# The first two modulation rows of an adaLN block: two halves of 512 columns in place of four blocks of 256

## The chip, the cores and the metric

The kernel runs on one core of a Trainium2 chip. The time is the device time in microseconds (us) of one execution. A profile is one execution recorded by the hardware profiler; its times count from the start of its span, and lines such as L142 are lines of the kernel before.

## The reference

One transformer block, x of 2048 rows and D = 1024 columns, all in bf16. A condition vector c makes six modulation rows, two of which, `sa` (shift) and `ca` (scale), are needed before anything else:

```python
mod = (_silu(c) @ w_mod).reshape(c.shape[0], 6, 1, -1)
sa, ca, ga, sb, cb, gb = (mod[:, 0].copy(), mod[:, 1].copy(), mod[:, 2].copy(), mod[:, 3].copy(), mod[:, 4].copy(), mod[:, 5].copy())
h = _layernorm(x, axis=-1) * (1 + ca) + sa
x = x + ga * _A_ref(h, A_wqkv, A_wo)          # linear attention, 32 heads of 32
h = _layernorm(x, axis=-1) * (1 + cb) + sb
x = x + gb * _B_ref(h, B_w_gate, B_w_up, B_w_down)   # SwiGLU, F = 3584
```

In `_A_ref` the keys and queries go through phi(t) = t + 1 for t > 0, exp(t) otherwise; `kv` and `z` are sums over all rows, so the keys and values of all of x come first.

## The kernel before

The 2048 rows are four chunks of 512, each of four tiles of 128. `M4` holds the normalized, transposed and modulated x: for each chunk eight column blocks (`cc`, 128 features on the partitions) of 512 rows. After the start that this text is about, the order is: values (`v_group`, L257) and queries (`q_group`, L265) of chunk 0, keys and values of chunks 1 to 3 with the sums `kv_mm` (L274), the other queries, attention output (L466), then gate and up (L509, L515) and down (L534). All of it is written out in a list of labelled steps (`seq`, `after`) and emitted in that order; engines run their own instructions strictly in that order, and waits between engines are semaphores. The schedule is manual: nothing reorders it.

The start, up to the first value matmul, is code ahead of that list. Its parts:

- **Loads, all on the queue of SyncE (SP), in order.** c, four tiles of x (`load_x`, L137, 256 KB each), then `load_wme` (L142) and `load_wk` (L145) in turn. `wme` is an SBUF region for the 2048 columns of `w_mod` that make `sa` (columns 0 to 1023) and `ca` (1024 to 2047); `load_wme(p)` brings the 256 columns p of each, in two transfers of 512 KB, whose rows in memory are 512 bytes. `wk` are the key weights, 2 MB in rows of 2 KB, cut by column block: 0 and 1, 2 and 3, 4 and 5, 6, 7. Behind them stand the values' weights (`load_cols`, L148), the next four tiles of x and the queries' weights. A transfer waits on SP for the landing of the transfer eight before it.
- **Layer norm of the four tiles.** VectorE takes the statistics (`ln_stats`, L196 to L200), GpSimd the reciprocal root (L202, L204); `ln_xn` writes the normalized tile, on ScalarE (L214) for tiles 0, 1 and 3 and on GpSimd (L211) for tile 2.
- **Transposes.** `tr0(st)` (L326) turns a tile over on TensorE, eight transposes into bank `st` of PSUM; `tr0_evac(st)` copies them to `M4`, on ScalarE (L332) for tiles 0 and 2, on VectorE (L334) for tiles 1 and 3.
- **Modulation.** `mod_mm(p)` (L343) makes 256 columns of `ca` and of `sa` as columns of PSUM bank 7, 32 matmuls of one column each; `mod_rows(p)` copies them on VectorE (L349, L350) and adds 1 to the scale (L351); `modulate` (L224, VectorE) applies both to one column block of `M4` in place.
- **Keys of chunk 0.** Eight groups `G` = (tile, half of 512 columns), each a sum over the eight column blocks in a bank of its own: `kmm` (L242) is one matmul of 512 columns. Since a block p of modulation rows serves only two column blocks, seven groups run side by side in banks 0 to 6: all seven over column blocks 0 and 1, then 2 and 3, then 4 and 5, with the next block's `mod_mm` between their matmuls (at k == 10), and last each group over 6 and 7, with its evacuation `k_evac` (phi, L237 to L239) behind it. Bank 7 belongs to the modulation until then; group 7 follows as a whole.
- `warm(n)` (L187) issues n matmuls on zeros into bank 7: 21 at the very start, 3 between the transposes of tiles 0 and 1.

Of the kernel before, what the change touches and what calls it, by code (L numbers as in the profile page):

```python
# [21 lines left out]
def kernel(  # L22
# [13 lines left out]
    nc = tc.nc  # L36
    P = nc.NUM_PARTITIONS
    _, S, D = A_x.shape
# [3 lines left out]
    DC = D // P  # L42
# [4 lines left out]
    STC = SCW // P  # L47
    NB = 512
# [18 lines left out]
    wm_v = w_mod.rearrange("(p j) n -> p j n", j=DC)  # L67
    c_v = c.rearrange("o (p j) -> p (o j)", j=DC)
# [8 lines left out]
    bank = [psum.tile([P, NB], F32, name=f"bank{i}") for i in range(8)]  # L77
# [9 lines left out]
    def view(region, off, shape, dtype=BF16):  # L87
        n = 1
        for s_ in shape:
            n *= s_  # L90
        w = n * (2 if dtype == F32 else 1)
        ap = region[:, off:off + w]
        if dtype == F32:
            ap = ap.bitcast(F32)
        if len(shape) == 2:
            ap = ap.rearrange("p (a b) -> p a b", a=shape[0])
        elif len(shape) == 3:
            ap = ap.rearrange("p (a b c) -> p a b c", a=shape[0], b=shape[1])
        return ap
# [6 lines left out]
    wme = view(M3, 0, [DC, 2 * D])  # L106
# [24 lines left out]


    c_sb = const.tile([P, DC], BF16, name="c_sb")
    nc.sync.dma_start(out=c_sb[:], in_=c_v)

    def load_x(st):
        nc.sync.dma_start(out=xs[st % 6], in_=x2[st * P:(st + 1) * P, :])  # L137

    def load_wme(p):
        for base in (D, 0):  # L140
            s_ = slice(base + p * 256, base + (p + 1) * 256)
            nc.sync.dma_start(out=wme[:, :, s_], in_=wm_v[:, :, s_])  # L142

    def load_wk(c0, c1):
        nc.sync.dma_start(out=wk[:, c0:c1, :], in_=wqkv_v[:, c0:c1, D:2 * D])  # L145

    def load_cols(dst, base, h):
        nc.sync.dma_start(out=dst[:, :, h * NB:(h + 1) * NB],  # L148
                          in_=wqkv_v[:, :, base + h * NB:base + (h + 1) * NB])

    for st in range(STC):
        load_x(st)
    load_wme(0)
    load_wk(0, 2)
    load_wme(1)
    load_wk(2, 4)
    load_wme(2)
    load_wk(4, 6)
    load_wme(3)
    load_wk(6, 7)  # L160
    load_wk(7, 8)

# [9 lines left out]
    saT = const.tile([P, DC], BF16, name="saT")  # L172
    ca1T = const.tile([P, DC], BF16, name="ca1T")
    sbT = const.tile([P, DC], BF16, name="sbT")
    cb1T = const.tile([P, DC], BF16, name="cb1T")
    m1 = const.tile([P, 6, DC], BF16, name="m1")
# [5 lines left out]
    scT = const.tile([P, DC], BF16, name="scT")  # L182
    nc.scalar.activation(out=scT[:], in_=c_sb[:], func=ACT.Silu)

    def warm(n):
        for _ in range(n):
            nc.tensor.matmul(bank[7][:], lhsT=zt[:, 0:P], rhs=zt[:], start=True, stop=True)  # L187
# [4 lines left out]
    def ln_stats(st):  # L192
        x_sb = xs[st % 6]
        stats = small.tile([P, NH, nc.vector.BN_STATS_DIM], F32, name="stats")
        for i in range(NH):
            nc.vector.bn_stats(out=stats[:, i, :], in_=x_sb[:, i * NB:(i + 1) * NB])  # L196
        mv = small.tile([P, nc.vector.BN_AGGR_DIM], F32, name="mv")
        nc.vector.bn_aggr(out=mv[:], in_=stats[:])
        veps = small.tile([P, 1], F32, name="veps")
        nc.vector.tensor_scalar_add(out=veps[:], in0=mv[:, 1:2], scalar1=LN_EPS)  # L200
        rstd = small.tile([P, 1], F32, name="rstd")
        nc.gpsimd.tensor_tensor(out=rstd[:], in0=veps[:], in1=neg_half[:], op=ALU.pow)  # L202
        nmr = small.tile([P, 1], F32, name="nmr")
        nc.gpsimd.tensor_scalar(out=nmr[:], in0=mv[:, 0:1], scalar1=rstd[:], scalar2=-1.0,  # L204
                                op0=ALU.mult, op1=ALU.mult)
        stat[st] = (rstd, nmr)

    def ln_xn(st, pool):
        rstd, nmr = stat.pop(st)
        if pool:  # L210
            nc.gpsimd.tensor_scalar(out=xns[st % 6], in0=xs[st % 6], scalar1=rstd[:], scalar2=nmr[:],  # L211
                                    op0=ALU.mult, op1=ALU.add)
        else:
            nc.scalar.activation(out=xns[st % 6], in_=xs[st % 6], func=ACT.Identity, scale=rstd[:], bias=nmr[:])  # L214
# [7 lines left out]
    def modulate(sc_, cc, sT, c1T, c0=0, c1=SCW):  # L222
        h = M4[:, sc_, cc, c0:c1]
        nc.vector.tensor_scalar(out=h, in0=h, scalar1=c1T[:, cc:cc + 1], scalar2=sT[:, cc:cc + 1],  # L224
                                op0=ALU.mult, op1=ALU.add)
# [9 lines left out]
    def phi_to(dst, acc):  # L235
        e = epool.tile([P, NB], F32, name="e")
        nc.scalar.activation(out=e[:], in_=acc, func=ACT.Exp)  # L237
        nc.vector.tensor_scalar(out=e[:], in0=e[:], scalar1=1.0, scalar2=PHI_EPS, op0=ALU.min, op1=ALU.add)  # L238
        nc.vector.scalar_tensor_tensor(out=dst, in0=acc, scalar=0.0, in1=e[:], op0=ALU.max, op1=ALU.add)  # L239

    def kmm(acc, sc_, t, h, cc):
        nc.tensor.matmul(acc[:], lhsT=M4[:, sc_, cc, t * P:(t + 1) * P], rhs=wk[:, cc, h * NB:(h + 1) * NB],  # L242
                         start=(cc == 0), stop=(cc == DC - 1))

    def k_evac(acc, t, h):
        phi_to(pk[:, t, h * NB:(h + 1) * NB], acc[:])
# [76 lines left out]
    def tr0(st):  # L323
        tp = bank[st][:].bitcast(BF16).rearrange("p (c s) -> p c s", c=DC)
        for cc in range(DC):
            nc.tensor.transpose(tp[:, cc, :], xns[st][:, cc * P:(cc + 1) * P], ident[:])  # L326

    def tr0_evac(st):
        tp = bank[st][:].bitcast(BF16).rearrange("p (c s) -> p c s", c=DC)
        dst = M4[:, 0, :, st * P:(st + 1) * P]  # L330
        if st % 2 == 0:
            nc.scalar.copy(out=dst, in_=tp)  # L332
        else:
            nc.vector.tensor_copy(out=dst, in_=tp)  # L334

    def mod_mm(p):
        mps = bank[7][:, p * 4:p * 4 + 4]
        for kind, base in enumerate((D, 0)):
            for i in range(2):
                col = base + (2 * p + i) * P  # L340
                o = kind * 2 + i
                for j in range(DC):
                    nc.tensor.matmul(mps[:, o:o + 1], lhsT=wme[:, j, col:col + P], rhs=scT[:, j:j + 1],  # L343
                                     start=(j == 0), stop=(j == DC - 1))

    def mod_rows(p):
        mps = bank[7][:, p * 4:p * 4 + 4]
        c2 = slice(2 * p, 2 * p + 2)
        nc.vector.tensor_copy(out=m1[:, 1, c2], in_=mps[:, 0:2])  # L349
        nc.vector.tensor_copy(out=saT[:, c2], in_=mps[:, 2:4])  # L350
        nc.vector.tensor_scalar_add(out=ca1T[:, c2], in0=m1[:, 1, c2], scalar1=1.0)  # L351

    warm(21)
    for st in range(STC):
        ln_stats(st)
    ln_xn(2, True)
    mask = const.tile([P, KVW], BF16, name="mask")
    nc.gpsimd.memset(mask[:], 0.0)
    for j in range(HPC):
# [7 lines left out]
    ln_xn(1, False)  # L367
    tr0(1)
    tr0_evac(0)
    tr0_evac(1)  # L370
    mod_mm(0)
    mod_rows(0)
    modulate(0, 0, saT, ca1T, 0, 2 * P)
    modulate(0, 1, saT, ca1T, 0, 2 * P)
    tr0(2)
    ln_xn(3, False)
    load_cols(wv, 2 * D, 0)
    for st in range(STC, STC + 4):
# [1 line left out]
    load_cols(wv, 2 * D, 1)  # L380
    load_cols(wq, 0, 0)
    load_cols(wq, 0, 1)

    tr0_evac(2)
    G = [(t, h) for t in range(STC) for h in range(NH)]
    for g in (0, 1):
        for cc in (0, 1):
            kmm(bank[g], 0, G[g][0], G[g][1], cc)
    tr0(3)
    tr0_evac(3)  # L390
    modulate(0, 0, saT, ca1T, 2 * P, 4 * P)
    modulate(0, 1, saT, ca1T, 2 * P, 4 * P)
    for g in (2, 3):
        for cc in (0, 1):
            kmm(bank[g], 0, G[g][0], G[g][1], cc)
    mod_mm(1)
    mod_rows(1)
    for g in (4, 5, 6):
        for cc in (0, 1):
            kmm(bank[g], 0, G[g][0], G[g][1], cc)  # L400
    modulate(0, 2, saT, ca1T)
    modulate(0, 3, saT, ca1T)
    for p in (1, 2):
        k = 0
        for cc in (2 * p, 2 * p + 1):
            for g in range(7):
                kmm(bank[g], 0, G[g][0], G[g][1], cc)
                k += 1
                if k == 10:
                    mod_mm(p + 1)  # L410
                    mod_rows(p + 1)
                    modulate(0, 2 * p + 2, saT, ca1T)
                    modulate(0, 2 * p + 3, saT, ca1T)
    for g in range(7):
        for cc in (6, 7):
            kmm(bank[g], 0, G[g][0], G[g][1], cc)
        k_evac(bank[g], *G[g])
    for cc in range(DC):
        kmm(bank[7], 0, G[7][0], G[7][1], cc)
    k_evac(bank[7], *G[7])  # L420


    seq = []
# [264 lines left out]
```

## Time and profile before

| what | time |
|---|---|
| median of 4 runs | 848.64 us (848.32 to 849.03) |
| the profiled execution | 849.02 us, its span 847.2 us |
| first value matmul (L257) | 33.03 us |
| last modulation transfer: issued, landed | 17.54 us, 26.66 us |
| key matmul (L242), median | 379 ns; 216 ns from start to start where they follow each other |
| 32 modulation matmuls (L343) in a row | 0.80 us |
| `modulate`, 256 columns and 512 columns | 334 ns and 406 ns |
| granted clock of TensorE, mean | 0.997 |

The chain of waits follows the end of the program back to its start: at each step to what released it. A window's sum gives each engine's busy time in a stretch, the clock that TensorE was granted (1.00 is full speed), the mean busy share of the 16 DMA engines and what they moved. A matmul's time is its length from issue to its last result; matmuls overlap, so their distance from start to start tells what one costs.

### The profile page before, as it was taken

What the parts mean: (1) busy time and instruction counts of PE and PEld (TensorE: products, weight loads), DVE (VectorE), ACT (ScalarE), POOL (GpSimd) and SP (SyncE); (2) the same over time, 40 slices, a digit from 0 to 9 for tenths busy, and PEclk for the clock granted to TensorE, in tenths of its full rate; (3) what the DMA queues carried; (4) which work ended last, traced back from release to release, by engine and by line L of the source; (5) the groups of instructions that cost most, each with busy time, mean ns of one, the idle gap of its engine ahead of it and who ended that gap; (6) DMA issues with size and microseconds to landing.
All of it is one profiled execution on the core that took longest, in us unless ns stands there. A gap on an engine that the chain in (4) does not pass through costs nothing.

```text
span 847.2 us, 10893 instructions
## 1 busy us (share of the span) xinstructions
PE 834.7 (99%) x4368; PEld 396.6 (47%) x4452; DVE 323.5 (38%) x617; ACT 143.9 (17%) x269; POOL 80.0 (9%) x143
## 2 busy tenths in 40 slices
PE   8999999999999999999999999999999999999998
PEld 4444555544444444444444444444444444444444
DVE  5657365497755655422111121221122122112222
ACT  3333233322311111111111001111000111100000
POOL 2124030014122323100000000000000000000000
PEclk9999999999999999999999999999999999999999
DMA  9994982045499898777886215555322555301220
GB/s 285 308 242 114 283 191 69 1 116 159 99 213 216 217 218 213 194 246 238 242 240 180 69 52 168 151 150 149 106 75 69 151 153 158 86 18 64 75 69 26
DMA packets 203763, 128.65 MB, mean 152 GB/s; under 512 B 50496, under 2 KB 189888, under 8 KB 203712
## 3 DMA queue, kind: packets, MB, share of 16 engines
q1 hardware_dynamic: 163008, 98.58, 40.9%
q10 hardware_dynamic: 38400, 20.98, 11.1%
q0 software_dynamic: 2304, 8.39, 2.6%
q8 instruction: 35, 0.57, 0.3%
q14 instruction: 16, 0.13, 0.1%
HBM read 103.81 MB, written 12.58 MB: 137 GB/s over the span
## 4 chain that ended last, share of the span: by engine, by line
PE 95%; SPq 2%; DVE 1%; DMA 1%; issue 1%; ACT 0%; DVEq 0%
PE bank L515 23%; PE bank L534 23%; PE bank L509 23%; PE bank L466 7%; PE bank L265 6%; PE bank L257 6%; PE bank L242 5%; DMA M<-in_w_mod_dram 1%; SPq L145 1%; PE bank L439 1%; PE bank L274 1%; SPq L142 1%; PE bank L301 1%; DVE stats L196 0%; DVE M L239 0%
## 5 line engine op out<-in xcount | busy, mean ns | idle before, releaser
L515 PE MATMUL bank<-M,M 128*128 128x512 bf16 x881 | 210.4, 379 | 0.8
L509 PE MATMUL bank<-M,M 128*128 128x512 bf16 x871 | 209.7, 379 | 1.3
L517 DVE TENSOR_TENSOR M<-bank,e 128x512 bf16<-128x512 f32 x112 | 77.5, 692 | 275.1 <-PE bank L515 265.7
L534 PE MATMUL bank<-M,M 128*128 128x512 bf16 (+1 forms) x687 | 146.9, 370 | 0.6
L512 ACT ACTIVATE e<-bank 128x512 f32<-128x512 f32 x112 | 66.8, 597 | 439.7 <-PE bank L509 422.0
L534 PEld LDWEIGHTS <-M 128*128 128x128 bf16 x924 | 90.4, 98 | 103.2
L515 PEld LDWEIGHTS <-M 128*128 128x128 bf16 x896 | 87.7, 98 | 105.7
L509 PEld LDWEIGHTS <-M 128*128 128x128 bf16 x896 | 87.3, 98 | 103.8
L538 DVE TENSOR_TENSOR M<-bank,gb_bc 128x512 f32<-128x512 f32 (+1 forms) x33 | 22.3, 676 | 149.2 <-PE bank L534 135.3
L242 PE MATMUL bank<-M,M 128*128 128x512 bf16 x244 | 58.5, 383 | 0.9 <-issue 0.2
L466 PE MATMUL bank<-M,M 128*128 128x512 bf16 x254 | 57.8, 379 | 0.1
L265 PE MATMUL bank<-M,M 128*128 128x512 bf16 x250 | 56.7, 379 | 0.3
L257 PE MATMUL bank<-M,M 128*128 128x512 bf16 x250 | 56.2, 379 | 0.3
L237 ACT ACTIVATE e<-bank 128x512 f32<-128x512 f32 x64 | 37.8, 598 | 100.7 <-PE bank L265 48.4
L534 PE MATMUL bank<-M 128*128 128x512 bf16 x219 | 50.7, 379 | 0.3
L239 DVE SCALAR_TENSOR_TENSOR M<-bank,e 128x512 bf16<-128x512 f32 x64 | 44.3, 692 | 3.7
L238 DVE TENSOR_SCALAR e<-e 128x512 f32<-128x512 f32 x64 | 27.8, 434 | 41.5 <-ACT e L237 41.5
L466 PEld LDWEIGHTS <-M 128*128 128x128 bf16 x256 | 25.0, 98 | 29.7
L257 PEld LDWEIGHTS <-M 128*128 128x128 bf16 x256 | 24.7, 98 | 29.0
L242 PEld LDWEIGHTS <-M 128*128 128x128 bf16 x256 | 24.4, 99 | 28.4 <-DVE M L224 1.3
L265 PEld LDWEIGHTS <-M 128*128 128x128 bf16 x256 | 24.6, 98 | 27.9
L468 DVE TENSOR_TENSOR M<-bank,M 128x512 f32<-128x512 f32 x32 | 22.1, 690 | 14.5 <-PE bank L466 14.3
(66 smaller groups left out, 335.6 us busy)
## 6 DMA issues: line engine op xcount, KB each, us to landing
M<-in_B_w_gate_dram SPq DMA_DIRECT2D x56, 512.0 KB, 3.9
M<-in_B_w_up_dram SPq DMA_DIRECT2D x56, 512.0 KB, 5.0
M<-in_w_mod_dram SPq DMA_DIRECT2D x8, 1024.0 KB, 6.6
x_scratch<-M POOLq DMA_DIRECT2D x16, 512.0 KB, 5.8
M<-x_scratch ACTq DMA_DIRECT2D x16, 512.0 KB, 3.5
M<-in_B_w_down_dram SPq DMA_DIRECT2D x6, 1024.0 KB, 7.9
M<-in_A_x_dram SPq DMA_DIRECT2D x16, 256.0 KB, 6.8
M<-in_w_mod_dram SPq DMA_DIRECT2D x8, 512.0 KB, 8.0
```

Source lines behind the costliest of these rows:

```text
L237: nc.scalar.activation(out=e[:], in_=acc, func=ACT.Exp)
L238: nc.vector.tensor_scalar(out=e[:], in0=e[:], scalar1=1.0, scalar2=PHI_EPS, op0=ALU.min, op1=ALU.add)
L239: nc.vector.scalar_tensor_tensor(out=dst, in0=acc, scalar=0.0, in1=e[:], op0=ALU.max, op1=ALU.add)
L242: nc.tensor.matmul(acc[:], lhsT=M4[:, sc_, cc, t * P:(t + 1) * P], rhs=wk[:, cc, h * NB:(h + 1) * NB], start=(cc == 0), stop=(cc == DC - 1))
L257: nc.tensor.matmul(acc[:], lhsT=M4[:, sc_, cc, t * P:(t + 1) * P], rhs=wv[:, cc, h * NB:(h + 1) * NB], start=(cc == 0), stop=(cc == DC - 1))
L265: nc.tensor.matmul(acc[:], lhsT=wq[:, cc, qc * P:(qc + 1) * P], rhs=M4[:, sc_, cc, :], start=(cc == 0), stop=(cc == DC - 1))
L466: nc.tensor.matmul(acc[:], lhsT=oTs[st % 3][:, cc, :], rhs=wo[:, cc, hs], start=(cc == 0), stop=(cc == DC - 1))
L509: nc.tensor.matmul(g_ps[:], lhsT=wg_blk[:, cc, fs], rhs=M4[:, sc_, cc, :], start=(cc == 0), stop=(cc == DC - 1))
L512: nc.scalar.activation(out=sg[:], in_=g_ps[:], func=ACT.Silu)
L515: nc.tensor.matmul(u_ps[:], lhsT=wu_blk[:, cc, fs], rhs=M4[:, sc_, cc, :], start=(cc == 0), stop=(cc == DC - 1))
L517: nc.vector.tensor_tensor(out=gus[sc_][:, f, :], in0=u_ps[:], in1=sg[:], op=ALU.mult)
L534: nc.tensor.matmul(y_ps[:, 0:w], lhsT=gus[sc_][:, f, t * P:(t + 1) * P], rhs=wd(f)[:, c0:c1], start=(f == 0), stop=(f == FC - 1))
```

## The change

The modulation columns are loaded and used in two halves of 512: scale columns and shift columns of column blocks 0 to 3, then of 4 to 7. A transfer is 1,024 KB with rows of 1 KB. The key weights keep their five transfers, two behind the first half and three behind the second. The first tile of x is issued ahead of c.

On the engines: `mod_mm` and `mod_rows` take scale and shift apart (`kind` 0 and 1). Tile 2 is normalized on ScalarE; `ln_xn(2, False)` and `ln_xn(3, False)` stand behind `tr0_evac(0)` and ahead of `tr0_evac(2)` on that engine. All four tiles are transposed before the first key matmul, and two warm matmuls stand between. Then groups 0 to 3 run over column blocks 0 to 3, groups 4 to 6 over the same with the second half's scale matmuls ahead of the last block, then come the second half's shift matmuls, group 7 over blocks 0 to 3 in bank 7, and last all eight groups over blocks 4 to 7, each with its evacuation. The number of key matmuls (64) and of modulation matmuls (128) is the same.

```diff
--- before.py
+++ after.py
@@ -131,15 +131,13 @@
 
 
     c_sb = const.tile([P, DC], BF16, name="c_sb")
-    nc.sync.dma_start(out=c_sb[:], in_=c_v)
 
     def load_x(st):
         nc.sync.dma_start(out=xs[st % 6], in_=x2[st * P:(st + 1) * P, :])
 
-    def load_wme(p):
-        for base in (D, 0):
-            s_ = slice(base + p * 256, base + (p + 1) * 256)
-            nc.sync.dma_start(out=wme[:, :, s_], in_=wm_v[:, :, s_])
+    def load_wme(base, half):
+        s_ = slice(base + half * NB, base + (half + 1) * NB)
+        nc.sync.dma_start(out=wme[:, :, s_], in_=wm_v[:, :, s_])
 
     def load_wk(c0, c1):
         nc.sync.dma_start(out=wk[:, c0:c1, :], in_=wqkv_v[:, c0:c1, D:2 * D])
@@ -148,15 +146,17 @@
         nc.sync.dma_start(out=dst[:, :, h * NB:(h + 1) * NB],
                           in_=wqkv_v[:, :, base + h * NB:base + (h + 1) * NB])
 
-    for st in range(STC):
+    load_x(0)
+    nc.sync.dma_start(out=c_sb[:], in_=c_v)
+    for st in range(1, STC):
         load_x(st)
-    load_wme(0)
+    load_wme(D, 0)
+    load_wme(0, 0)
     load_wk(0, 2)
-    load_wme(1)
     load_wk(2, 4)
-    load_wme(2)
+    load_wme(D, 1)
+    load_wme(0, 1)
     load_wk(4, 6)
-    load_wme(3)
     load_wk(6, 7)
     load_wk(7, 8)
 
@@ -333,27 +333,25 @@
         else:
             nc.vector.tensor_copy(out=dst, in_=tp)
 
-    def mod_mm(p):
-        mps = bank[7][:, p * 4:p * 4 + 4]
-        for kind, base in enumerate((D, 0)):
-            for i in range(2):
-                col = base + (2 * p + i) * P
-                o = kind * 2 + i
-                for j in range(DC):
-                    nc.tensor.matmul(mps[:, o:o + 1], lhsT=wme[:, j, col:col + P], rhs=scT[:, j:j + 1],
-                                     start=(j == 0), stop=(j == DC - 1))
-
-    def mod_rows(p):
-        mps = bank[7][:, p * 4:p * 4 + 4]
-        c2 = slice(2 * p, 2 * p + 2)
-        nc.vector.tensor_copy(out=m1[:, 1, c2], in_=mps[:, 0:2])
-        nc.vector.tensor_copy(out=saT[:, c2], in_=mps[:, 2:4])
-        nc.vector.tensor_scalar_add(out=ca1T[:, c2], in0=m1[:, 1, c2], scalar1=1.0)
+    def mod_mm(kind, c0, c1):
+        for cc in range(c0, c1):
+            o = (2 * cc) + kind
+            col = (0 if kind else D) + cc * P
+            for j in range(DC):
+                nc.tensor.matmul(bank[7][:, o:o + 1], lhsT=wme[:, j, col:col + P], rhs=scT[:, j:j + 1],
+                                 start=(j == 0), stop=(j == DC - 1))
+
+    def mod_rows(kind, c0, c1):
+        src = bank[7][:, 2 * c0 + kind:2 * c1 + kind:2]
+        if kind:
+            nc.vector.tensor_copy(out=saT[:, c0:c1], in_=src)
+        else:
+            nc.vector.tensor_copy(out=m1[:, 1, c0:c1], in_=src)
+            nc.vector.tensor_scalar_add(out=ca1T[:, c0:c1], in0=m1[:, 1, c0:c1], scalar1=1.0)
 
     warm(21)
     for st in range(STC):
         ln_stats(st)
-    ln_xn(2, True)
     mask = const.tile([P, KVW], BF16, name="mask")
     nc.gpsimd.memset(mask[:], 0.0)
     for j in range(HPC):
@@ -367,12 +365,7 @@
     ln_xn(1, False)
     tr0(1)
     tr0_evac(0)
-    tr0_evac(1)
-    mod_mm(0)
-    mod_rows(0)
-    modulate(0, 0, saT, ca1T, 0, 2 * P)
-    modulate(0, 1, saT, ca1T, 0, 2 * P)
-    tr0(2)
+    ln_xn(2, False)
     ln_xn(3, False)
     load_cols(wv, 2 * D, 0)
     for st in range(STC, STC + 4):
@@ -380,44 +373,42 @@
     load_cols(wv, 2 * D, 1)
     load_cols(wq, 0, 0)
     load_cols(wq, 0, 1)
-
+    mod_mm(0, 0, 4)
+    tr0(2)
+    tr0_evac(1)
     tr0_evac(2)
+    mod_rows(0, 0, 4)
+    warm(2)
+    for c0 in (0, 2):
+        mod_mm(1, c0, c0 + 2)
+        mod_rows(1, c0, c0 + 2)
+        if c0 == 0:
+            tr0(3)
+        for cc in (c0, c0 + 1):
+            modulate(0, cc, saT, ca1T, 0, 2 * P)
+    tr0_evac(3)
+    for cc in range(4):
+        modulate(0, cc, saT, ca1T, 2 * P, 4 * P)
     G = [(t, h) for t in range(STC) for h in range(NH)]
-    for g in (0, 1):
-        for cc in (0, 1):
+    for cc in range(4):
+        for g in range(4):
             kmm(bank[g], 0, G[g][0], G[g][1], cc)
-    tr0(3)
-    tr0_evac(3)
-    modulate(0, 0, saT, ca1T, 2 * P, 4 * P)
-    modulate(0, 1, saT, ca1T, 2 * P, 4 * P)
-    for g in (2, 3):
-        for cc in (0, 1):
+    for cc in range(4):
+        for g in range(4, 7):
             kmm(bank[g], 0, G[g][0], G[g][1], cc)
-    mod_mm(1)
-    mod_rows(1)
-    for g in (4, 5, 6):
-        for cc in (0, 1):
-            kmm(bank[g], 0, G[g][0], G[g][1], cc)
-    modulate(0, 2, saT, ca1T)
-    modulate(0, 3, saT, ca1T)
-    for p in (1, 2):
-        k = 0
-        for cc in (2 * p, 2 * p + 1):
-            for g in range(7):
-                kmm(bank[g], 0, G[g][0], G[g][1], cc)
-                k += 1
-                if k == 10:
-                    mod_mm(p + 1)
-                    mod_rows(p + 1)
-                    modulate(0, 2 * p + 2, saT, ca1T)
-                    modulate(0, 2 * p + 3, saT, ca1T)
-    for g in range(7):
-        for cc in (6, 7):
+        if cc == 2:
+            mod_mm(0, 4, 8)
+            mod_rows(0, 4, 8)
+    mod_mm(1, 4, 8)
+    mod_rows(1, 4, 8)
+    for cc in range(4, 8):
+        modulate(0, cc, saT, ca1T)
+    for cc in range(4):
+        kmm(bank[7], 0, G[7][0], G[7][1], cc)
+    for g in range(8):
+        for cc in range(4, 8):
             kmm(bank[g], 0, G[g][0], G[g][1], cc)
         k_evac(bank[g], *G[g])
-    for cc in range(DC):
-        kmm(bank[7], 0, G[7][0], G[7][1], cc)
-    k_evac(bank[7], *G[7])
 
 
     seq = []
```

## The prediction

> **What bounds the kernel now.** I read the page's busy shares first, then the chain of waits over the first 60 us, then the sums by window for the DMA rate and the granted clock, then the timeline.
>
> ```profile
> span 847.2 us, 10893 instructions
> PE 834.7 (99%) x4368; PEld 396.6 (47%) x4452; DVE 323.5 (38%) x617; ACT 143.9 (17%) x269; POOL 80.0 (9%) x143
> ```
>
> TensorE is busy 99% of the span, so the change can only move what TensorE waits for before it streams. That is the start. The chain of waits, columns start, length, what:
>
> ```profile
> 16.95 0.54 SPq L142
> 17.50 0.04 issue
> 17.54 9.11 DMA M<-in_w_mod_dram
> 26.66 0.05 issue
> 26.70 0.55 PE bank L343 x16
> 27.25 0.89 PE bank L242 x4
> 28.14 0.03 issue
> 28.17 1.36 PE bank L242 x5
> 29.52 0.05 issue
> 29.58 3.62 PE bank L242 x16
> 33.19 7.12 PE bank L257 x33
> ```
>
> The last quarter of the two modulation rows is issued at 17.54 and lands at 26.66; behind it stand 16 modulation matmuls, a short wait for `modulate`, and the last key matmuls. From L257 on (the values of chunk 0; the timeline has the first at 33.03) the chain is TensorE without a gap of any size, to the end. So the change is worth what it does to one number, **the start of the first value matmul, now 33.03 us**. Nothing after it is edited: the same number of transfers, in the same order, follows.
>
> The whole start is fed by one stream of transfers. Columns below: window, length, busy us of PE, PEld, DVE, ACT, POOL (with counts), granted clock, DMA share, GB/s.
>
> ```profile
> 6.00:23.00 17.00, 14.76 (x166) 8.81 (x166) 9.03 (x29) 6.91 (x6) 5.18 (x19) 0.90 1.13 317
> 54.00:61.00 7.00, 6.95 (x34) 3.17 (x33) 6.29 (x17) 2.44 (x5) 0.00 (x0) 1.00 1.07 353
> 9.63:13.04 3.41, 1.82 (x46) 1.65 (x47) 2.95 (x9) 2.02 (x2) 2.54 (x7) 1.00 1.14 322
> 13.04:16.46 3.42, 3.20 (x19) 1.97 (x18) 0.38 (x1) 2.29 (x2) 0.63 (x9) 0.50 1.13 328
> ```
>
> A DMA share over 1 means that the queue is full: the stream runs at its own speed. In 6 to 23 us it moves rows of 512 bytes (modulation) and 2 KB (key weights); in 54 to 61 us it moves the late modulation loads of L293, rows of 1 KB from the same tensor, and is faster. The last two rows are for the clock, below.
>
> **The change, part by part.**
>
> *1. Rows of 1 KB.* The three late loads of L293 are issued at 50.54, 51.19 and 51.90 and land after 6.7, 9.1 and 11.3 us, at 57.2, 60.3 and 63.2: 3.0 us for each MB (1,024 KB). The rows before: the second load of block 0 lands at 10.67 (issued 3.77, 6.9 us), that of block 3 at 26.66. In these 16.0 us three blocks and three 512 KB pieces of key weights pass. A key piece takes 1.5 us at 353 GB/s (0.524 MB), which makes 4.5; one 16 KB instruction fetch lies in the queue near 17.4 us, and its packet lasts 1.2. That leaves 10.3 us, 3.43 for each MB. Saved: 0.43 to 0.45 a MB, for four MB **1.8 us**.
> Here a rule can be weighed against the row. The Trainium skill, "DMA: Bandwidth & Descriptors", section "Why small descriptors are slow (HBM only)", charges about 3 cycles for each packet on top of 32 bytes a cycle. By that 512 bytes cost 19 cycles and 1 KB costs 35, and a MB would go from 3.43 to 3.43 × 35/38 = 3.16 us: an estimate of 1.1 us saved in all. The sum below would come out at 848.8 in place of 848.1. I take the row: same tensor, same rows, same queue.
>
> *2. Order.* The last modulation piece now has one 512 KB key piece less ahead of it (1.0 MB in place of 1.5), 1.5 us. It lands at 26.66 − 1.8 − 1.5 = **23.35**. The last key rows, L145, land now at 27.96 (issued 23.36, 4.6 us); they gain only the 1.8, **26.15**. The first half lands later than block 0 did: its scale row at 10.67 − 0.45 = 10.2, its shift row 3.0 later at 13.2.
>
> *3. What follows the last modulation piece.* 32 matmuls of one column take 0.80 us (17.25 to 18.05 in the timeline). The copy of the row starts 0.20 after the last one and takes 0.16; bank 7 is free 0.06 later: 0.05 + 0.78 + 0.42 = 1.25 from landing. Four key matmuls into bank 7 (0.216 each, start to start) give 0.86, under which the four `modulate` of 512 columns run (0.33 apart, first from 1.25). The fourth is ready at 2.7 and its first user comes at 2.76, so nothing is left over. Then 32 key matmuls, 6.9. Sum: landing + 9.0 = **32.35**. This is longer than the 6.37 us behind the last landing now, since four column blocks of all eight groups wait in place of two of seven and a whole group.
>
> *4. The last key rows.* Group 0 needs column block 7 at once: 26.15 + 0.05 + 29 matmuls × 0.216 = **32.46**.
>
> *5. The first half on TensorE.* c_v moves behind the first tile of x: that tile is issued 0.45 earlier, and the normalization with it, except that the 21 warm matmuls end at 8.19 as now. Tile 2's normalization moves from GpSimd to ScalarE, behind the copy of tile 0's transposes and ahead of tile 3's: copy until about 10.1, then 1.24 and 1.24 more, ending near 11.3 and 12.6. So the 32 scale matmuls run 10.25 to 11.05, tile 2's transposes to 11.8, the two warm matmuls to 12.2, then a wait for 13.2. Shift matmuls, tile 3's transposes, shift matmuls: to 14.5 (14.9 with the transposes at half clock). The key matmul into bank 3 waits for VectorE, where two row copies, four `modulate` of 256 columns (0.33) and the 0.69 us copy of tile 3 are queued in that order: 16.4 to 16.75. Three key matmuls fit in ahead of it. The four remaining `modulate` end by 18 and are covered by 13 key matmuls (2.8 us). From there 22 key matmuls 4.75, 32 scale matmuls 0.80 (their half landed near 20.4), three key matmuls 0.65: TensorE is at the last shift row at **22.65 to 22.95**, 0.4 to 0.7 before it lands. With no wait at all this path would give 31.65 to 31.95.
>
> *6. Small parts.* The four fewer transfers cost nothing on SP, which is not late. The eight evacuations come every 0.86 us while VectorE needs 1.06 for each (29.54 to 30.61 in the timeline); the last ends near 36 us, now 38.1; bank 4, the last that a value group claims, is free long before its turn. The values' weights land now at 32.1, 0.9 us before use; they move up by 1.8 as well.
>
> **Sum.** The latest of 31.95, 32.35 and 32.46 sets the start: 32.46 − 33.03 = −0.57 us. The profiled execution took 849.02 (span 847.2 and 1.8 around it), and would be 848.45; the median of the runs is 848.64, 0.38 lower than that execution, and the difference goes off it: **848.1 us**. A measurement of this kernel can tell about 0.2%, 1.7 us, from no change; this is inside.
>
> **The rivals.**
>
> *A. One half-clock window more.* The row 9.63 to 13.04 holds 32 one-column matmuls, 14 transposes and a 1.4 us gap, and the next 3.42 us ran at 0.50. The Trainium skill, "TensorE: Matmul & The Clock Gate", section "HAM oscillation", gives as its rule no gaps over about 3.4 us; by that the new order, with no gap over 1.1 us, would never slow down. The row contradicts it, and speaks against this change: here the gap was 1.4. Between 21.2 and 24.5 the new kernel has 64 one-column matmuls, about a microsecond of waiting and only three key matmuls, a mix like that of the throttled row. A half-clock window there costs 3.41/2 = 1.7 us, fully on the path: 849.8. If instead the early one lasts past 16.4, to 19.9, TensorE is 1.7 late and the landing hides 0.4 to 0.7: about 849.2. Both are within 0.2%.
>
> *B. The slower side: the half clock holds for two windows behind the second half.* 3.4 us lost, 851.5. It decides when more than 1.7 + 0.57 = 2.3 us are lost, 1.35 windows. Against it: once the key matmuls flow, one busy window lifted it at 16.46.
>
> *C. The rows don't help.* If 1 KB rows go no faster at this crowded place, the last shift row lands at 25.15, plus 9.0: 34.15, 849.8. Against it: the row of 54 to 61 us.
>
> *D. The faster side.* The engine that the fetch delays by 1.2 us is what lands last. If the fetch falls elsewhere, shift row and key rows land at 22.1 and 24.9, and the first half too comes up to a microsecond sooner (shift row 12.2, TensorE ready at 21.9): 22.1 + 9.0 = 31.1, −1.9 us, 846.7.
>
> **How the numbers follow.** Forecast 0.48 (own range 847.3 to 849.0), A 0.15, C 0.08, B 0.16, D 0.13. Same: 0.48 + 0.15 + 0.08 = 0.71; slower 0.16; faster 0.13. The range reaches from D's 846.5 to the upper end of A and C, 850.2, and leaves out B.
>
> **What would show it.** First L257 matmul near 32.5; last shift row landing near 23.4 and the last key rows near 26.1; DMA about 350 GB/s from 6 to 24 us; granted clock 1.0 from 20 us on. I am wrong if the clock is 0.5 anywhere behind 20 us, if TensorE reaches the last shift row after it has landed, or if the landings haven't moved.

## The result

| | before | changed |
|---|---|---|
| median | 848.69 us (52 runs) | 849.85 us (34 runs) |
| lowest and highest | 848.12 to 849.31 | 848.04 to 850.89 |
| ratio, 95% interval | | 1.0012, 1.0007 to 1.0017 |
| profiled execution, its span | 849.02, 847.2 | 849.49, 847.7 |
| first value matmul | 33.03 | 33.23 |

The changed kernel is slower by 0.12%. That is less than the 0.2% that I had called the limit of what can be told, but clear of its interval: the forecast of 848.1 missed by 1.75 us, and in sign. The spread is as telling: the kernel before stays within 1.2 us, the changed one covers 2.9. Grouped by the mean granted clock that each execution reports, the 34 fall apart:

```
mean granted clock    executions    median us
0.997 and 0.998            9          848.78
0.995 and 0.996           25          850.07
```

One stretch of 3.41 us at half clock lowers the mean over 847 us by 0.002, so the second row is one such stretch more, and it comes with 1.3 us. The page of the changed kernel's profile has almost the same busy shares as before:

```profile
span 847.7 us, 10891 instructions
PE 834.6 (98%) x4370; PEld 396.5 (47%) x4454; DVE 323.0 (38%) x614; ACT 145.4 (17%) x270; POOL 78.9 (9%) x142
```

The chain of waits of the changed kernel's first 60 us (start, length, what; L341 is now the modulation matmul, L347 the copy of a shift row):

```profile
3.77 10.00 DMA M<-in_w_mod_dram
13.77 0.05 issue
13.82 0.59 PE bank L341 x16
14.40 0.88 PE bank L326 x8
...
16.52 0.61 DVE M L334
17.13 0.04 issue
17.17 2.36 PE bank L242 x6
...
22.99 0.78 PE bank L341 x32
23.77 0.45 PE bank L242 x2
24.22 0.05 issue
24.27 0.96 PE bank L341 x32
...
29.35 4.05 PE bank L242 x18
33.40 6.69 PE bank L257 x31
```

The last landing that the chain follows is now that of the **first** half's shift row, 13.77. The second half's landed at 22.96 and no one was waiting: from 17.17 on the chain is TensorE, but for the copy of the last shift row, and TensorE comes to that row at 24.27, 1.3 us after it landed. The landing of that row, issued at 9.65 (L140):

```profile
DMA to landing us min/median/max: 13.3/13.3/13.3
```

Sums by window of the changed kernel (columns as in the prediction: PE, PEld, DVE, ACT, POOL busy, clock, DMA share, GB/s):

```profile
3.00:6.00 3.00, 3.00 (x10) 1.06 (x9) 2.22 (x5) 0.21 (x1) 0.64 (x2) 1.00 0.76 217
6.00:23.00 17.00, 14.36 (x141) 7.92 (x141) 8.36 (x26) 7.90 (x7) 3.57 (x17) 0.80 1.07 358
12.21:19.04 6.83, 5.41 (x50) 2.85 (x49) 3.24 (x11) 2.65 (x3) 0.28 (x3) 0.50 1.08 365
```

The clock is 0.50 for 6.83 us, twice as long as before, and a tile's transposes, 0.45 us at full clock (tile 2), take 0.88 in the chain. Of the 1.3 us, half clock from the key matmul at 17.17 to 19.04 makes 0.9. The other 0.4 was there before: that matmul, the first into bank 3, was forecast for 16.75 at the latest, and the first half's shift row for 13.2. The stream did what was forecast from 6 us on, 358 GB/s against 317. Behind the start nothing moved: the delay of 0.20 us at the first value matmul (33.03 and 33.23) is 0.20 at VectorE's last pass but one (843.85 and 844.05).

### The profile page after: what moved, and what is told of

Read it like the earlier page. It is cut to its first block, busy times and chain, and to the rows that moved or that the text cites. A ratio compares the mean times of both kernels' runs of the same rounds, so it can differ in the third digit from the quotient of the medians.

```text
span 847.7 us, 10891 instructions
## 1 busy us (share of the span) xinstructions
PE 834.6 (98%) x4370; PEld 396.5 (47%) x4454; DVE 323.0 (38%) x614; ACT 145.4 (17%) x270; POOL 78.9 (9%) x142
## 4 chain that ended last, share of the span: by engine, by line
PE 96%; DVE 2%; DMA 1%; issue 1%; SPq 0%; ACT 0%; DVEq 0%
PE bank L506 23%; PE bank L525 23%; PE bank L500 23%; PE bank L457 7%; PE bank L265 6%; PE bank L257 6%; PE bank L242 6%; DMA M<-in_w_mod_dram 1%; PE bank L430 1%; PE bank L274 1%; PE bank L301 1%; DVE stats L196 0%; DVE M L239 0%; PE bank L341 0%; DVE e L238 0%
```

## The experiments

The confidence intervals here are those of each run's own comparison with the kernel before; "clock" is the mean granted clock of an execution. Diffs are against the changed kernel unless another is named; "..." marks what is left out. Where a diff shifts the lines, value matmuls are L256, modulation matmuls L340 and key matmuls L241.

**e1_fill: the waits filled.**

```diff
-    warm(3)
+    warm(5)
     ln_xn(1, False)
...
+    warm(4)
     mod_mm(0, 0, 4)
...
-    warm(2)
+    warm(7)
```

> The changed kernel with its waits filled by matmuls on zeros: warm(5) in place of warm(3) ahead of tile 1's transposes, warm(4) ahead of the first scale matmuls, warm(7) in place of warm(2). Theory (the half clock costs the time): TensorE has no gap over 0.5 us before 15 us, the granted clock stays 1.00 behind 6 us or loses one window at most, TensorE is at the last shift row at about 23.0 us as it lands, the first value matmul starts near 32.1 (33.24 in the profile of the changed kernel), and the median is 0.8 to 1.7 us below the changed kernel's 849.85: 848.1 to 849.0. Rival (the longer tail behind the last landing costs it, whatever the clock): the first value matmul stays at 33.2 or later and the median at 849.5 to 850. Rival (filling is itself too slow: at half clock 7 fillers take 3.0 us): 850.5 or more.

Median 848.84; ratio 1.0000 (0.9992 to 1.0008). All 13 executions have a clock of 0.999 or 1.000. The full microsecond that the change had cost is gone, with no other edit, so the rivals of the longer tail and of the slow fillers fall. In its profile the last shift row landed at 23.87, TensorE came to it at 24.00, and the first value matmul started at 32.88, 9.0 us after the landing. The sum from 6 to 23 us, and the chain where it comes to that row:

```profile
6.00:23.00 17.00, 15.00 (x169) 8.55 (x170) 8.02 (x25) 8.02 (x7) 3.54 (x17) 1.00 1.04 346
23.41 0.59 PE bank L242 x2
24.00 0.88 PE bank L341 x32
24.88 0.02 issue
24.90 0.17 DVE saT L347
```

My 32.1 for that start had assumed the landing at about 23.0; in this execution all modulation rows landed 0.7 to 0.9 later than in the changed kernel's profile. So the median is the witness here: the two profiles differ by only 0.35 us.

**e2_nowarm: without the two warm matmuls ahead of the shift rows.**

```diff
-    warm(2)
     for c0 in (0, 2):
```

> The changed kernel without the two warm matmuls ahead of the shift rows. Theory (half clock): the gap before the shift matmuls is 1.7 us in place of 1.2, so the clock is halved for two windows in nearly every execution: median 850.0 to 850.6. Rival (the clock costs nothing, the tail does): no change, 849.85 within 0.2. A second rival (two fillers only delay): 849.5.

Median 849.77, ratio 1.0013 (1.0004 to 1.0021): not told apart from the changed kernel's 849.85, under the range of the theory, and where the first rival put it. That rival's reason, a clock that costs nothing, falls with e1_fill. Eleven of 13 executions were at 0.996 or below, against 25 of 34 of the changed kernel; the one at 0.994 took 852.31. Two fillers neither helped nor hurt measurably.

**e3_old_loads: the new computation, the old loads.**

```diff
... (load_wme as in the kernel before)
-    load_wme(D, 0)
-    load_wme(0, 0)
+    load_wme(0)
     load_wk(0, 2)
+    load_wme(1)
     load_wk(2, 4)
-    load_wme(D, 1)
-    load_wme(0, 1)
+    load_wme(2)
     load_wk(4, 6)
+    load_wme(3)
```

> The new order of the computation with the old loads: four blocks of 256 columns, in rows of 512 bytes, in the old sequence between the key weights. The rows of the second half land at about 25.1 (scale) and 26.7 (shift) in place of 20.1 and 23.0. Step 3 of the sum says that 9.0 us follow the last landing: first value matmul at 35.6 to 35.7, 2.4 us later than in the profile of the changed kernel, median near 851.3 to 852.3, whatever the clock does before 20 us. If TensorE's own pace sets the end and the landing is hidden: no change, 849.9.

Median 851.48, ratio 1.0035 (1.0024 to 1.0045), inside the range. The shift rows landed at 26.49 and the first value matmul started at 35.11, 8.6 us later; half of the shift columns were there earlier, and 16 of the 32 matmuls were already done. So the new order taken alone is worse by 2.7 us than the kernel before (848.76 beside it), and the new loads win back about 1.6 us of that.

**e4_before_fill: the kernel before with its gap filled.** Against the kernel before:

```diff
     modulate(0, 1, saT, ca1T, 0, 2 * P)
+    warm(5)
     tr0(2)
```

> The kernel before with warm(5) in its 1.4 us gap ahead of tile 2's transposes. Theory: the half-clock window of the kernel before lies under the wait for the last modulation landing (26.66), so removing it gains nothing: the clock is 1.00 from 6 us on, the first value matmul stays at 33.0, median 848.7 within 0.3. Rival (a window at half clock costs 1.7 us in any place of the start): 847.0 to 847.5.

Median 848.75, ratio 0.9998 (0.9990 to 1.0006). Twelve of 13 executions have 0.999 or 1.000; the profiled one is the thirteenth. The kernel before loses a half-clock window in about three executions of four (99 of the 136 beside these experiments are below 0.999) and pays nothing that can be measured: whatever TensorE is late with there waits for the landing at 26.66 anyway. The same loss in the new order is in the open.

**e5_c_first: c ahead of x again.**

```diff
-    load_x(0)
     nc.sync.dma_start(out=c_sb[:], in_=c_v)
-    for st in range(1, STC):
+    for st in range(STC):
         load_x(st)
```

> The changed kernel with c loaded ahead of the first tile of x again, as in the kernel before. Theory (the small rows of c, put between tiles of x, slow the start of the stream): the DMA rate from 3 to 6 us is back at about 350 GB/s from 217, tile 3 of x lands near 6.4 in place of 7.9, every later landing is 0.5 to 1 us sooner, and the last shift row lands near 22.3. TensorE still meets two half-clock windows, so only part of it arrives: median 849.2 to 849.6, against 849.85. Rival (c's place costs nothing, the slow start was chance): no change in the rate beyond one execution, median 849.85.

Median 849.70, ratio 1.0010 (1.0002 to 1.0019): just outside the expected range, and not resolved from 849.85. But its profile happens to be an execution in which the clock was never halved (0.999), and shows what the sum had described. Its chain:

```profile
22.67 0.05 issue
22.72 0.97 PE bank L340 x32
23.69 0.03 issue
23.71 0.17 DVE saT L346
...
31.86 6.69 PE bank L256 x31
```

The last shift row lands at 22.67, TensorE is waiting for it, and the first value matmul starts at 31.69. The execution took 847.95. The rate from 3 to 6 us is back at 339 GB/s, but the landing is only 0.3 us sooner than in the changed kernel's profile, and in that of e2_nowarm, with c behind the first tile, the same row landed at 22.48, sooner still.

**e6_fill_c_first: both.** The diffs of e1_fill and e5_c_first together.

> Both repairs: the waits filled as in e1_fill, and c ahead of x. Theory: e1_fill (848.84) is bound by the landing of the shift rows alone, so the 0.5 to 0.8 us of the stream arrive in full: median 848.1 to 848.4, and with it the forecast of the sum. Rival (c's place costs nothing): 848.8, as e1_fill.

Median 848.66, ratio 1.0003 (0.9996 to 1.0009), 0.3 above the upper end of what I expected. The eight executions at 1.000 have a median of 848.23, the nine at 0.999 one of 848.58, and four at 0.997 or 0.998 lie at 849.98 to 851.18. The profile is one of the four:

```profile
21.43:24.84 3.41, 2.99 (x70) 2.12 (x70) 1.07 (x5) 0.00 (x0) 0.00 (x0) 1.00 1.07 372
24.84:28.25 3.41, 3.41 (x10) 1.22 (x8) 1.05 (x4) 0.60 (x1) 0.00 (x0) 0.50 1.08 366
```

This is the late window of rival A: behind the 64 modulation matmuls of the second half the clock is halved, with 32 key matmuls in a row to come. The first value matmul was at 33.73, 10.7 us behind the landing (23.03): 9.0 and the 1.7 for one window. TensorE counts as busy for 2.99 of the 3.41 us before it, so being busy by the profile's count did not protect it.

**e7_evac_act: and tile 3's copy on ScalarE.** Against e6_fill_c_first:

```diff
-        if st % 2 == 0:
+        if st != 1:
             nc.scalar.copy(out=dst, in_=tp)
```

> e6_fill_c_first with the copy of tile 3's transposes on ScalarE, which is idle there, in place of behind the modulation on VectorE. Theory: the stall of 0.5 to 0.8 us ahead of the key matmul into bank 3 goes, TensorE is at the last shift rows about 0.6 us earlier, but then waits for them to land near 22.5: gain 0 to 0.4 us on e6, median 847.9 to 848.3. Rival (TensorE's own path is what is last, not the landing): 0.6 us on e6.

Median 849.50, ratio 1.0007 (0.9999 to 1.0015), over a microsecond above the range. Seven executions at 0.999 or 1.000 have medians of 848.04 and 847.95, which is what was expected; six at 0.997 or 0.998 lie at 849.5 to 850.45. TensorE now arrives earlier and waits longer, and a window is lost in six of 13 executions, against four of 21; that is too few to call it more often. With the clock full, 9.0 us lie behind the landing once more (22.77 to 31.79).

**e8_loads_alone: the new loads, the old computation.** The kernel before with the new `load_wme(base, half)` and the new sequence of loads, c first.

> The kernel before with the new loads alone: modulation columns in two halves of 512 with 1 KB rows and key weights in the new sequence, c first, all computation as before. Block 0 then waits for both rows of a whole half (13.2 in place of 10.7), and TensorE has a gap of about 2.5 us there. By step 1 the last shift row lands at 22.5 to 23.4 in place of 26.66, and 6.4 us lie behind that landing, but blocks 2 and 3 then come together and 26 key matmuls and 32 columns still follow block 2: first value matmul near 33.2 with a full clock and 33.5 to 34.5 with two half-clock windows: median 848.9 to 850. Rival (the faster rows alone carry the gain): first value matmul at 32 or before, median 847.7 or less.

Median 850.23, ratio 1.0020 (1.0012 to 1.0028), 0.2 above the range; no execution is above 0.998. Its first value matmul was at 34.67. The new loads alone make it worse: block 0 then waits for half of all columns (a landing at 13.72 in its chain, 10.67 before), and from there on the chain is TensorE. The rival falls. How much of the loss is the late block and how much the clock, halved for at least one window in every execution, is not shown.

**e9_spread: a denser second half.** Against e7_evac_act:

```diff
+        if cc in (1, 2):
+            mod_mm(0, 2 * cc + 2, 2 * cc + 4)
         if cc == 2:
-            mod_mm(0, 4, 8)
             mod_rows(0, 4, 8)
+    warm(3)
     mod_mm(1, 4, 8)
```

> e7_evac_act with a denser second half: the 32 scale matmuls of column blocks 4 to 7 are cut in two, after six and after nine of the twelve key matmuls of groups 4 to 6, and three matmuls on zeros stand ahead of the shift matmuls, in the time in which their rows are awaited. Theory (a stretch of one-column matmuls counts as idle for the clock, so e6 and e7 lose a window behind 24 us in some executions): the clock is 0.999 or 1.000 in nearly all executions (7 of 13 for e7), first value matmul near 31.8 to 32.2, median 848.0 to 848.3, 0.3 to 0.7 below the kernel before. Rival (the window is lost to the wait for the landing, not to the one-column matmuls, or whatever one does): the same split as e7, median 849 to 849.5.

All 13 executions have 0.999 or 1.000, median 848.36; the kernel before had 848.89 beside it. Ratio 0.9995, 0.9986 to 1.0003: the clock came out as expected, the gain over the kernel before is not resolved. One execution at 1.000 took 850.70, so the clock does not account for every slow one; no profile shows what does.

```profile
23.08 0.05 issue
23.12 0.97 PE bank L340 x32
24.09 0.02 issue
24.11 0.17 DVE saT L346
24.29 0.04 issue
24.33 7.94 PE bank L241 x36
32.27 7.77 PE bank L256 x36
```

Key matmuls run without a break behind the copy, and the first value matmul is at 32.10, again 9.0 behind the landing.

**e10_before_x_first: c behind the first tile, in the kernel before.** Against the kernel before:

```diff
+    load_x(0)
     nc.sync.dma_start(out=c_sb[:], in_=c_v)
-    for st in range(STC):
+    for st in range(1, STC):
         load_x(st)
```

> The kernel before with one edit: c is loaded behind the first tile of x. Theory (its rows of 16 bytes between tiles of x slow the stream): rate from 3 to 6 us near 220 to 300 GB/s in place of 354, and since 6.4 us follow the last modulation landing with nothing to hide it, the median rises by 0.3 to 0.8 us, to 848.9 to 849.4. Rival (no cost): 848.6 within 0.15.

Median 849.09 beside 848.89, ratio 1.0003 (0.9994 to 1.0011): a cost of 0.2 us is possible and not resolved. The rate from 3 to 6 us is 240 GB/s:

```profile
3.00:6.00 3.00, 3.00 (x9) 1.08 (x8) 1.65 (x4) 0.21 (x1) 0.51 (x1) 1.00 0.88 240
```

Over all kernels of this study, one profile each, this rate is 217 to 273 GB/s in the five with c behind the first tile and 296 to 354 in the nine with c first. The two groups don't overlap. The landings do: here the last modulation row landed at 26.68, and at 26.66 before; with the new loads it is 22.48, 22.96 and 23.87 with c behind the first tile and 22.67 to 23.55 in the six with c first.

**e11_one_column: other fillers in the same gap.** Against e4_before_fill:

```diff
-    warm(5)
+    for _ in range(40):
+        nc.tensor.matmul(bank[7][:, 500:501], lhsT=zt[:, 0:P], rhs=zt[:, 0:1], start=True, stop=True)
     tr0(2)
```

> e4_before_fill with its five full matmuls replaced by 40 matmuls of one column, about 1.0 us of TensorE by the profile's busy time, the same as the five. Theory (one-column matmuls count as idle for the clock): the clock of most executions is 0.996 to 0.998 as in the kernel before (62 of 86 executions beside the earlier experiments), against 12 of 13 at 0.999 or 1.000 for e4. Rival (any busy TensorE counts): 0.999 or 1.000 as e4. The time is 848.6 within 0.3 either way.

Median 848.53, ratio 0.9997 (0.9989 to 1.0005). Eleven of 13 executions are at 0.997 or 0.998 and two at 1.000, much as in the kernel before (23 of 33 beside it below 0.999); with five full matmuls in the same place it was one of 13 below 0.999. The stretch ahead of the halved one in its profile:

```profile
9.27:12.68 3.41, 2.82 (x82) 2.38 (x80) 3.23 (x10) 2.29 (x3) 2.50 (x5) 1.00 1.08 329
12.68:16.09 3.41, 3.04 (x18) 1.93 (x18) 0.41 (x1) 2.31 (x3) 1.33 (x11) 0.50 1.13 324
```

TensorE is busy for 2.82 of 3.41 us, 83%, and the clock is halved all the same. Matmuls of one column, 72 of them, make 2.06 us of that.

**e12_split_only: e9_spread without its three fillers.** The line `warm(3)` of e9 taken out.

> e9_spread without the three matmuls on zeros ahead of the last shift matmuls; the scale matmuls stay cut in two. If the split alone keeps the second half dense enough, the clock is 0.999 or 1.000 in nearly all executions and the median is that of e9, 0.3 to 0.7 us below the kernel before. If the wait ahead of the shift rows, with nothing in it, tips a window, about half of the executions are at 0.997 or 0.998, as for e7, and the median is 849 or above. I take the first for somewhat likelier.

Eleven of 13 executions at 0.999 or 1.000, two at 0.997 with 850.3 and 850.6; median 848.37 beside 848.66, ratio 0.9999 (0.9991 to 1.0007). The count lies between the 7 of 13 of e7_evac_act and the 13 of 13 of e9_spread, and differs clearly from neither. That split and fillers together keep the clock is shown; the share of each is not.

## Why the prediction was wrong

**The step that failed is step 5**, "TensorE is at the last shift row at 22.65 to 22.95, 0.4 to 0.7 before it lands". It allowed half clock for the transposes of tile 3 and full clock from 16.4 us on. In the profile the half clock lasted to 19.04 and TensorE arrived at 24.27, 1.3 us behind the landing: 0.9 by the clock after 17.17, 0.4 from before. From there the sum's own tail holds: 24.27 + 9.0 = 33.27 against 33.23. Filling the gaps and nothing else (e1_fill) removes the microsecond that the change had cost, so this cause is shown, not only argued.

This is rival A, which I had given 0.15, in its early form: the window lasts past 16.4. I had priced that at 849.2 and the late window at 849.8, so that the median of 849.85 meets the price of the late one is luck. Of my three signs of being wrong one came, TensorE at the last shift row after its landing; the clock was full again at 19.04, and the landings had moved.

The clock is not the whole miss. With it full, e1_fill is at 848.84, still 0.7 above the forecast, and that rest has no cause shown. The first half's shift row may be part of it: forecast for 13.2, it landed between 13.15 and 14.71 in the nine with the new loads, whichever place c had.

**Why I had the clock wrong.** I had set the rule of the Trainium skill ("TensorE: Matmul & The Clock Gate", section "HAM oscillation"), no gaps over about 3.4 us, against the row with a 1.4 us gap, and said myself that the mix of one-column matmuls and waiting between 21 and 24.5 resembled that row. Then the sum went on at full clock. e11_one_column shows what a one-column matmul is worth to the clock: 40 of them protect no better than an empty gap, five full ones do. Counted so, the changed kernel has from about 10 us (end of tile 1's transposes) to 15.5 (first key matmul) only two tiles of transposes and two fillers, and a full clock there was unlikely: e5_c_first, with the same computation, had one in two of 13 executions. The trace of before could have told more: in the row ahead of its halved one, one-column matmuls are busy for 1.09 of the 1.82 us.

**Point by point.** *1, rows of 1 KB*: right. 358 GB/s from 6 to 23 us where 353 was taken from the late loads. By the 3 cycles for each packet of the Trainium skill ("DMA: Bandwidth & Descriptors", section "Why small descriptors are slow (HBM only)") a MB would have taken an estimated 3.16 us in place of 3.0; the two rows of the first half land at 10.79 and 13.77, 2.98 apart, on the side of the row. *2, order*: right; last shift row 22.96 (forecast 23.35), last key rows 25.68 (26.15), first half 10.79 and 13.77 (10.2 and 13.2). *3, nine microseconds behind the landing*: right to 0.1 in the three profiles with a full clock and the landing last (e5, e7, e9), and in e1, where TensorE comes 0.1 after the landing. *4, key rows*: not reached in the changed kernel; in e5 the two paths tie, since the last key rows land at 25.39 and step 4 puts 6.3 behind them. *5*: wrong as said, and in a smaller thing: the swap of c and the first tile of x was counted as a gain of 0.45 us that nobody needs. In this profile the first tile did land 0.5 sooner (3.36, from 3.87), but the fourth took 5.3 us from its issue in place of 3.8, and landed at 7.9 in place of 6.4. *6*: right, nothing of it shows; the shift at the start arrives unchanged at the end.

```profile
DMA to landing us min/median/max: 5.3/5.3/5.3
```

(The line is from the instructions of L136 in the changed kernel, the fourth tile alone.)

**The other rivals.** B, two windows behind the second half, was seen in no profile. C falls with the rate. D's price, 846.7, was not reached by any execution of any kernel here; the lowest was 847.63. The forecast's own number does appear with a full clock, but with c first: 847.95 and 848.11 for e5 at 0.999, 848.23 for e6 at 1.000.

**What stays open.** Whether the repaired kernel (e9_spread) beats the one before: its median was 0.5 us lower, its interval includes none. What the place of c costs from end to end: the rate from 3 to 6 us differs, but the landings overlap, the medians of e5 and e10 moved by 0.15 and 0.2 us, and with a full clock e1_fill (13 executions, 848.84) and e6_fill_c_first (17, 848.34) differ by 0.5; none of these is resolved. How much full work in a window keeps the clock was not tested, but three profiles bound it for a stretch without transposes. These are the key matmuls alone in the window with the second half's modulation matmuls (PE and PEld busy, clock, DMA share, GB/s), of e6_fill_c_first, e12_split_only and the changed kernel:

```profile
21.43:24.84 3.41, 1.26 (x6) 0.60 (x7) 1.00 1.07 372
21.52:24.94 3.42, 1.31 (x6) 0.50 (x6) 1.00 1.07 375
22.45:25.86 3.41, 1.52 (x7) 0.55 (x7) 1.00 1.08 367
```

The first two were followed by a halved window, the third was not; TensorE as a whole was busy for 2.99, 2.51 and 3.10 us. Three windows make no rule. That the outcome differs from execution to execution fits windows that lie differently each time (one ends at 12.21 in one profile here, at 12.68 in another), but no run sets their place.

## What to carry to other kernels

Ask of every stretch that hides something what it hides. The kernel before lost the clock too and paid nothing, since a landing held everything up; a change that brings that landing forward uncovers the slow clock beneath, and has to be costed at it. And count matmuls of a single column as gaps when the clock is at stake: spread between full ones, with fillers in the wait, they cost no window in 13 executions (e9_spread), and in one piece with nothing in the wait six of 13 (e7_evac_act).

## What the runs showed of the hardware that I had not expected

- Matmuls of one column count as busy in the profile (2.06 of the 2.82 busy us in a window of 3.41) and don't keep the clock: 11 of 13 executions with 40 of them in the gap lost a window, one of 13 with five full matmuls.
- A half-clock window on the critical path costs 1.7 us as computed (33.73 in place of 32.03 in e6), and moves whole executions: 848.78 and 850.07 for the two groups of the changed kernel.
- The transfer of c, 2 KB in rows of 16 bytes, went with a slower stream around it: 217 to 273 GB/s with c between tiles of x, 296 to 354 with c first, for three microseconds. Why is not shown, nor that any later landing moves with it.
